# Attention's long step: attention-value products ahead of the mask products, bits compared in two halves, the second weight operation between them

## The chip, the cores and the metric

The kernel runs on one core of a Trainium2 chip. The metric is the device time of one execution in microseconds; the time before is the median of three runs. Engines are named as in the profile: PE is TensorE (PEld its weight loads), DVE is VectorE, ACT is ScalarE, POOL is GpSimd, SP is SyncE, which issues most of the transfers. The core has its own PSUM of eight banks, into which only TensorE's products go.

## What is computed

Attention over 2 x 8 heads, 768 positions and 64 numbers per head, in which a query sees a key only if both fall into the same bucket; the bucket is the set of signs of six projections. Two feed-forward blocks follow (squared ReLU, then SiLU), each with 512 inputs and 2048 hidden units.

```python
q_bits = (np.einsum('bhsd,dk->bhsk', q, proj) > 0).astype(np.int64)
k_bits = (np.einsum('bhsd,dk->bhsk', k, proj) > 0).astype(np.int64)
...
mask = q_bucket[:, :, :, None] == k_bucket[:, :, None, :]
scores = scale * np.matmul(q, k.transpose(0, 1, 3, 2))
scores = np.where(mask, scores, -1000000000.0)
...
return np.matmul(attn, v).astype(np.float32)
...
h = np.maximum(x @ w_in, 0.0)
return (h * h @ w_out).astype(np.float32)
...
g = h * (1.0 / (1.0 + np.exp(-h)))
return (g @ w_out).astype(np.float32)
```

## The kernel before

**The stages.** Attention comes first, then the two feed-forward blocks, whose order is set by a planner (`Plan`, `moe`) that the change does not touch. Attention is written out by hand: `manual_schedule` keeps every engine's instructions in the order in which the loop over `d` (L890) issues them. Each engine works its own list in order and waits at an instruction whose inputs aren't there.

**Units of work.** Heads are taken in pairs `p` (8 of them), a pair has four units `u` (head and half of the queries), a unit three groups of 128 queries `j`. A step `d` works on several stages at once. In the order of the loop:

- `row_max` (L683, VectorE) reads the scores that the step before produced, and `row_live` (L687, L688) prepares the scale and bias of the exponential.
- `t_lo` (L722, VectorE) and `t_hi` (L716, ScalarE) split a transposed tile of probabilities into a high and a low part. `transp` (L711, TensorE) makes the transposed tiles, two per step, three transposes each.
- `mid` holds VectorE's operations on the first block's weights, which arrive as 64-bit words: `w_exp` (L641) cuts the exponent to size, `w_sign` (L645) puts the sign in, `w_low` (L649) the low word. Before `w_exp`, `w_abs` runs on ScalarE (L633) and `w_limit` on GpSimd (L637).
- `score_exp` (L696, ScalarE) reads the scores out of PSUM and frees their buffer.
- `av` (L735, L736, TensorE) multiplies the values with the split probabilities, twice per step, two products each, for tiles that were transposed four tiles earlier. At a unit's end ScalarE copies the result out (L741).
- `score_mm` (L678, TensorE) computes the next scores in four products, two of which take the bits of the mask as further rows of queries and keys.

**The long steps.** `extra` adds work to eight of the steps. In steps 5, 17, 29, 41, 53, 65 and 77 `bits_mm` (L521) makes the six projections of the next pair's queries and keys, twelve products of 48 rows (six for each half `z` of the positions), into a tile `bs`. `bits_cmp` (L526, VectorE) compares them with zero and writes the bits `bt`. In steps 17 to 77, and alone in step 92, `rb_mm` (L758) transposes the reciprocals of an earlier pair's sums, and `x_norm` (L767, VectorE) multiplies the attention's output with them. The tiles `s`, `bs` and `rb` share two PSUM buffers (`ps_s`): the bit products wait until the exponential has read the one, the reciprocal transposes until it has read the other, and in steps 17 to 77 the step's own score products take the buffer of `bs` once the comparison has read it.

**Behind the comparison.** `place_bits` (L602) has SyncE copy the twelve bit rows to the operands `qq` and `kk` of the pair's first head right in the long step. The scores that need them are those of two steps later. GpSimd issues the loads of the pair after that (`load_hi`, L484 and L485); the second takes the place of the data that the bit products read.

**In a long step before the change** the loop issues all products of `extra` ahead of `av`, the comparison behind them, and the normalisation behind `av`; all weight operations of `mid` stand at the step's start. `mid` has three of them in step 17 (exponent, sign, low word), two in steps 29, 53 and 77 (exponent, sign), one in steps 41 and 65 (low word), none in steps 5 and 92.

Of the kernel before, what the change touches and what calls it, by code (L numbers as in the profile page):

```python
# [17 lines left out]
ALU = mybir.AluOpType  # L18
# [8 lines left out]
QW = 384  # L27
# [406 lines left out]
def lsh_attention_moe_moe(ctx, tc, kd, qk, v, pc, wi1, wo1, wi2, wo2, out):  # L434
    nc = tc.nc
# [31 lines left out]
    tm = [pcr[:, 2 * PW + 24 + 2 * i : 2 * PW + 26 + 2 * i] for i in range(3)]  # L467
# [46 lines left out]
    def bits_mm(p):  # L514
# [6 lines left out]
                mm(s[0:48, z, 0:QW], w, x[:, z * QW : (z + 1) * QW], start=j == 0, stop=j == 5)  # L521
        return s

    def bits_cmp(s, p):
        bt = pair[p]["bt"] = a1.tile([128, S], F32R, tag="bt", name=f"bt{p}")
        nc.vector.tensor_scalar(  # L526
            out=bt[0:48].rearrange("p (a b) -> p a b", a=2),
            in0=s[0:48, :, 0:QW],
            scalar1=tm[0][0:48, 0:1],
            scalar2=tm[0][0:48, 1:2],  # L530
            op0=ALU.is_gt,
            op1=ALU.mult,
        )


    first = {}
# [134 lines left out]
    def score_mm(u, j):  # L671
        p, h, z = u // 4, (u // 2) % 2, u % 2
        t = pair[p]
        s = ps_s.tile([128, 2, 512], F32, tag="s", name=f"s{u}_{j}")
        c0 = z * QW + j * 128
        for ab, kk in ((0, 128), (1, 64 + NBR)):
            for n in range(2):
                mm(s[:, n, 0:QW], t["qq"][h][0:kk, ab, c0 : c0 + 128], t["kk"][h][0:kk, ab, n * QW : (n + 1) * QW], start=ab == 0, stop=ab == 1)  # L678
        return s

    def row_max(u, j, s):
        m = mt[:, (u * 3 + j) % 4]
        nc.vector.tensor_reduce(out=m[:, 0:1], in_=s[:, :, 0:QW], op=ALU.max, axis=AX.XY, negate=True)  # L683
        return m

    def row_live(m):
        nc.vector.tensor_scalar(out=m[:, 1:2], in0=m[:, 0:1], scalar1=LIM, scalar2=1.0, op0=ALU.is_lt, op1=ALU.mult)  # L687
        nc.vector.tensor_scalar(out=m[:, 2:3], in0=m[:, 0:1], scalar1=LIM, scalar2=m[:, 0:1], op0=ALU.is_lt, op1=ALU.mult)  # L688

    def score_exp(u, j, s, m):  # L690
        p = u // 4
        if u % 4 == 0 and j == 0:
            sums[p] = a2.tile([128, 12], F32, tag="sums", name=f"sums{p}")
        e = P[u, j] = ac.tile([128, S], F32, tag="P", bufs=6, name=f"P{u}_{j}")
        c = (u % 4) * 3 + j
        nc.scalar.activation(  # L696
            out=e.rearrange("p (a b) -> p a b", a=2),
            in_=s[:, :, 0:QW],
            func=AF.Exp,
            scale=m[:, 1:2],  # L700
            bias=m[:, 2:3],
            accum_out=sums[p][:, c : c + 1],
        )
# [3 lines left out]
    def transp(g):  # L707
        u, kt = divmod(g, KT)
        t = ps_t.tile([128, 512], F32, tag="t", name=f"t{g}")
        for j in range(3):  # L710
            nc.tensor.transpose(t[:, j * 128 : (j + 1) * 128], P[u, j][:, kt * 128 : (kt + 1) * 128], ident)  # L711
        PT[g] = (t,)

    def t_hi(g):
        th = a1.tile([128, QW], F32R, tag="th", bufs=6, name=f"th{g}")
        nc.scalar.copy(out=th, in_=PT[g][0][:, 0:QW])  # L716
        PT[g] += (th,)

    def t_lo(g):
        t, th = PT[g]  # L720
        tl = a1.tile([128, QW], F32R, tag="tl", bufs=6, name=f"tl{g}")
        nc.vector.tensor_tensor(out=tl, in0=t[:, 0:QW], in1=th.bitcast(F32), op=ALU.subtract)  # L722
        PT[g] = th, tl
# [3 lines left out]
    def av(g):  # L727
        u, kt = divmod(g, KT)
        p, h, z = u // 4, (u // 2) % 2, u % 2
        if kt == 0:  # L730
            otile[u] = ps_o.tile([128, 512], F32, tag="o", name=f"o{u}")
        o = otile[u]
        vv = pair[p]["vv"][:, h * KT + kt].rearrange("p a d -> p (a d)")
        th, tl = PT.pop(g)
        mm(o[:, 0:QW], vv, th, start=kt == 0, stop=False)  # L735
        mm(o[:, 0:QW], vv, tl, start=False, stop=kt == KT - 1)  # L736
        if kt == KT - 1:
            if p not in xs:
                xs[p] = [a1.tile([128, S], F32, tag=n, bufs=b, name=f"{n}{p}") for n, b in (("ta", 2), ("tb", 1))]
            ob = a2.tile([128, QW], F32, tag="ob", name=f"ob{u}")  # L740
            nc.scalar.copy(out=ob, in_=o[:, 0:QW])  # L741
            for i in range(2):
                nc.sync.dma_start(out=xs[p][i][64 * h : 64 * h + 64, z * QW : (z + 1) * QW], in_=ob[64 * i : 64 * i + 64])
# [44 lines left out]
    extra = defaultdict(list)  # L788
    mid = defaultdict(list)
# [48 lines left out]
    with tc.manual_schedule():  # L838
# [12 lines left out]
        def warm_up(n):  # L851
            for _ in range(n):
                mm(warm, zb[:, 0:128], zb[:, 0:512], start=True, stop=True)
# [36 lines left out]
        for d in range(-5, G // 2 + 3):  # L890
            ready, new = new, None
            g = 2 * d
            if ready:
                m = row_max(*ready)
            if 0 <= g - 1 < G:
                t_lo(g - 1)
            if ready:
                row_live(m)
            for fn, a in mid.pop(d, []):
                fn(a)  # L900
            if 0 <= g < G:
                transp(g)
                t_hi(g)
                t_lo(g)
                transp(g + 1)
                t_hi(g + 1)
            more = extra.pop(d, [])
            if ready and more:
                score_exp(*ready, m)
            held = [(dve, pe(p), p) for pe, dve, p in more]  # L910
            for dve, t, p in held[:1]:
                dve(t, p)
            for n in (g - V_LAG, g + 1 - V_LAG):
                if 0 <= n < G:
                    av(n)
            for dve, t, p in held[1:]:
                dve(t, p)
            if ready and not more:
                score_exp(*ready, m)
            u, j = divmod(d + 5, 3)  # L920
            if u < NU:
                new = u, j, score_mm(u, j)
            if d < -1:
                warm_up(2)
            for fn, a in todo.pop(d, []):
                fn(*a)
# [3 lines left out]
        p = NPAIR - 1  # L930
        for z in range(2):
            t = ps_t.tile([128, 512], F32, tag="t", name=f"rb{p}_{z}")
# [13 lines left out]
        t = dict(x0=x0, ys=ys, xa=xa, wp=wp, raw=raw, wt=wt, src=((wi1, wo1), (wi2, wo2)), out=out)  # L946
# [51 lines left out]
```

## Time and profile before

| | |
|---|---|
| Median of three runs | 764.95 us (762.88 to 766.0) |
| Profiled execution | 764.35 us, its span 762.6 us |
| Busy: PE, PEld, DVE, ACT, POOL | 742.7, 627.7, 598.5, 456.8, 406.2 us |
| Chain that ended last, by engine | PE 74%, DVE 17%, DMA 3%, ACT 2%, issue 2% |
| Granted TensorE clock, mean | 0.998 |

The span goes from the first to the last instruction. A busy time adds up an engine's instructions, whose ends overlap the starts of the next; two numbers of a timeline row are the start and the duration, so the distance to the next start is what an instruction costs in a full queue. The bracket at a row's end tells how long the engine had been idle and what released it. Attention ends at about 255 us of the span.

### The profile page before, as it was taken

The page shows a single profiled execution, that of the slowest core. Times are in us where ns is not written, and L with a number is a line of the kernel's source. Part 1 is how long each engine was busy: PE and PEld are TensorE (multiplying, and loading weights), DVE is VectorE, ACT ScalarE, POOL GpSimd, SP SyncE. Part 2 cuts the span into 40 slices and gives each one's busy share as a digit, 9 for nine tenths or more (in the row PEclk, how much of TensorE's full clock was granted, in tenths as well). Part 3 has the DMA queues.
Part 4 walks back from the last instruction along what each step waited for, and adds up shares of the span by engine and source line. Part 5 has one row for each costly group of instructions (what it writes and reads, how often), then busy time and mean ns, then how long its engine had stood idle before and what let it go on. Part 6 is the DMA issues. An engine that isn't in the chain of part 4 may idle for free.

```text
span 762.6 us, 10898 instructions
## 1 busy us (share of the span) xinstructions
PE 742.7 (97%) x3748; PEld 627.7 (82%) x3748; DVE 598.5 (78%) x1064; ACT 456.8 (60%) x856; POOL 406.2 (53%) x295
## 2 busy tenths in 40 slices
PE   7989999999999989999999999999999999999998
PEld 3688988989988878888888888888788888888887
DVE  4989999999999899658748966899975875685542
ACT  4777978888979766367268239446634625623520
POOL 3454464863754674753564662867567256455200
PEclk9999999999999999999999999999999999999999
DMA  5496976876851402221221211102222031121012
GB/s 150 127 230 162 218 186 162 212 201 154 217 124 36 168 28 83 83 83 56 83 79 60 83 58 50 61 28 80 88 83 83 25 113 32 53 93 45 1 69 97
DMA packets 29398, 77.09 MB, mean 101 GB/s; under 512 B 4432, under 2 KB 8912, under 8 KB 29344
## 3 DMA queue, kind: packets, MB, share of 16 engines
q1 hardware_dynamic: 25152, 64.99, 29.2%
q0 software_dynamic: 4032, 11.01, 6.2%
q8 instruction: 30, 0.49, 0.3%
q10 hardware_dynamic: 160, 0.39, 0.2%
q14 instruction: 24, 0.20, 0.1%
HBM read 52.15 MB, written 3.15 MB: 73 GB/s over the span
## 4 chain that ended last, share of the span: by engine, by line
PE 74%; DVE 17%; DMA 3%; ACT 2%; issue 2%; POOL 1%; SPq 1%; DVEq 0%; ACTq 0%
PE bank L336 32%; PE bank L255 16%; PE bank L226 9%; PE s L678 5%; DVE mt L683 4%; PE t L711 4%; DVE tl L722 3%; PE o L735 2%; PE o L736 2%; DVE ys L149 2%; PE bs L521 2%; ACT P L696 1%; DVE xb L155 1%; DVE ts L260 1%; DMA ta<-ob 1%
## 5 line engine op out<-in xcount | busy, mean ns | idle before, releaser
L170 POOL TENSOR_SCALAR wt<-wt 128x512 f32<-128x512 f32 x56 | 117.1, 2100 | 45.2 <-ACT wt L168 45.2
L155 POOL TENSOR_TENSOR wp<-wt,wp 128x512 fp32r<-128x512 f32 x56 | 76.6, 1379 | 96.1 <-ACT wp L153 96.1
L255 PE MATMUL bank<-xb,wp 128*128 128x512 f32 x480 | 111.3, 390 | 2.4 <-DVE ts L260 1.6
L696 ACT ACTIVATE P<-s,mt 128x768 f32<-128x768 f32 x96 | 95.6, 996 | 23.6 <-DVE mt L688 20.9
L255 PEld LDWEIGHTS bank<-xb,wp 128*128 128x128 f32 x480 | 89.7, 188 | 22.6 <-issue 1.5
L722 DVE TENSOR_TENSOR tl<-t,th 128x384 fp32r<-128x384 f32 x192 | 104.7, 547 | 1.8 <-ACT th L716 1.6
L683 DVE TENSOR_REDUCE mt<-s 128x1 f32<-128x768 f32 x96 | 91.3, 951 | 8.7 <-PE s L678 8.3
L153 ACT CAST wp<-wt 128x512 fp32r<-128x512 f32 x56 | 34.6, 620 | 105.7 <-DVE wt L173 64.4
L716 ACT CAST th<-t 128x384 fp32r<-128x384 f32 x192 | 82.2, 483 | 22.4 <-PE t L711 22.3
L678 PE MATMUL s<-kk,qq 76*128 76x384 f32 (+1 forms) x384 | 85.2, 341 | 6.1 <-DMA kk<-bt 2.1
L711 PE MATMUL t<-ident,P 128*128 128x128 f32 x576 | 81.7, 274 | 2.0 <-DVE tl L722 1.9
L260 DVE TENSOR_TENSOR ts<-bank,ts 128x512 f32<-128x512 f32 x80 | 54.5, 690 | 36.8 <-PE bank L255 34.2
L226 PE MATMUL bank<-x0h,wp 128*128 128x512 f32 x256 | 80.2, 389 | 0.0
L678 PEld LDWEIGHTS s<-kk,qq 76*128 76x128 f32 (+1 forms) x384 | 67.6, 188 | 10.2 <-issue 5.4
L711 PEld LDWEIGHTS t<-ident,P 128*128 128x128 f32 x576 | 67.6, 140 | 10.1 <-DVE tl L722 4.3
L735 PE MATMUL o<-th,vv 128*128 128x384 f32 x192 | 72.4, 377 | 0.1
L736 PE MATMUL o<-tl,vv 128*128 128x384 f32 x192 | 64.6, 337 | 0.0
L240 ACT ACTIVATE ts<-bank 128x512 f32<-128x512 f32 x48 | 28.6, 595 | 52.1 <-PE bank L226 26.6
L226 PEld LDWEIGHTS bank<-x0h,wp 128*128 128x128 f32 x256 | 48.1, 188 | 10.0
L155 DVE TENSOR_TENSOR gql<-ts,gqh 128x512 fp32r<-128x512 f32 x64 | 46.2, 733 | 12.7 <-ACT gqh L153 12.4
L172 DVE SCALAR_TENSOR_TENSOR wt<-raw,wt 128x512 uint32<-128x512 uint32 x58 | 51.5, 890 | 0.6
L168 ACT ACTIVATE wt<-raw 128x512 f32<-128x512 f32 x58 | 38.7, 669 | 20.6 <-POOL wp L155 11.0
(153 smaller groups left out, 1707.1 us busy)
## 6 DMA issues: line engine op xcount, KB each, us to landing
raw<-in_dram SPq DMA_DIRECT2D x64, 512.0 KB
qq<-hq SPq DMA_DIRECT2D x28, 192.0 KB
kk<-in_dram POOLq DMA_DIRECT2D x14, 384.0 KB, 5.0
vr<-in_dram SPq DMA_DIRECT2D x8, 384.0 KB
ta<-ob SPq DMA_DIRECT2D x32, 96.0 KB
tb<-ob SPq DMA_DIRECT2D x32, 96.0 KB
out_dram<-ts SPq DMA_DIRECT2D x11, 256.0 KB
rq<-in_dram SPq DMA_DIRECT2D x7, 384.0 KB
```

The lines of the kernel that those rows point to most:

```text
L155: add(("DVE", "POOL")[pool], l, lambda: eng.tensor_tensor(out=lo(), in0=src(), in1=hi().bitcast(F32), op=ALU.subtract), (*rk, *hk), lk)
L170: add("DVE" if fast else "POOL", 0.5 if fast else 2.4, lambda: eng.tensor_scalar(out=wtt, in0=wtt, scalar1=W_LO, scalar2=W_HI, op0=ALU.max ...
L226: mm(bank[b], w[:, x, op, sl], t["x0"][y][:, kt], start=kt == 0 and j == 0, stop=kt == 3 and j == 2)
L255: mm(bank[b], w[:, p, op, k * 128 : k * 128 + 128], x[:, q, xop, k], start=first and k == 0 and j == 0, stop=k == 1 and j == 2, skip_group ...
L336: mm(bank[b][:, 0:wd], x, y, start=i == 0 and n == 0, stop=i == FB - 1 and n == 2)
L678: mm(s[:, n, 0:QW], t["qq"][h][0:kk, ab, c0 : c0 + 128], t["kk"][h][0:kk, ab, n * QW : (n + 1) * QW], start=ab == 0, stop=ab == 1)
L683: nc.vector.tensor_reduce(out=m[:, 0:1], in_=s[:, :, 0:QW], op=ALU.max, axis=AX.XY, negate=True)
L696: nc.scalar.activation(out=e.rearrange("p (a b) -> p a b", a=2), in_=s[:, :, 0:QW], func=AF.Exp, scale=m[:, 1:2], bias=m[:, 2:3], accum_ou ...
L711: nc.tensor.transpose(t[:, j * 128 : (j + 1) * 128], P[u, j][:, kt * 128 : (kt + 1) * 128], ident)
L716: nc.scalar.copy(out=th, in_=PT[g][0][:, 0:QW])
L722: nc.vector.tensor_tensor(out=tl, in0=t[:, 0:QW], in1=th.bitcast(F32), op=ALU.subtract)
L735: mm(o[:, 0:QW], vv, th, start=kt == 0, stop=False)
```

## The change

`av` comes ahead of the products of `extra`, so that in a long step the order on TensorE is transposes, attention-value products, bit products, reciprocal transposes, scores. Both kinds of `extra` work are now issued as products first and VectorE work behind them. The comparison becomes two instructions of 384 columns, one per half of the positions. In a long step the weight operations of `mid` from the second on are kept back in a list `between` and issued after the first half.

```diff
+    between = []
+
     def bits_cmp(s, p):
         bt = pair[p]["bt"] = a1.tile([128, S], F32R, tag="bt", name=f"bt{p}")
-        nc.vector.tensor_scalar(
-            out=bt[0:48].rearrange("p (a b) -> p a b", a=2),
-            in0=s[0:48, :, 0:QW],
-            scalar1=tm[0][0:48, 0:1],
-            scalar2=tm[0][0:48, 1:2],
-            op0=ALU.is_gt,
-            op1=ALU.mult,
-        )
+        for z in range(2):
+            nc.vector.tensor_scalar(
+                out=bt[0:48, z * QW : (z + 1) * QW],
+                in0=s[0:48, z, 0:QW],
+                scalar1=tm[0][0:48, 0:1],
+                scalar2=tm[0][0:48, 1:2],
+                op0=ALU.is_gt,
+                op1=ALU.mult,
+            )
+            while between:
+                fn, a = between.pop(0)
+                fn(a)
...
             if ready:
                 row_live(m)
-            for fn, a in mid.pop(d, []):
-                fn(a)
+            more = extra.pop(d, [])
+            for i, (fn, a) in enumerate(mid.pop(d, [])):
+                if more and i:
+                    between.append((fn, a))
+                else:
+                    fn(a)
             if 0 <= g < G:
                 transp(g)
                 t_hi(g)
                 t_lo(g)
                 transp(g + 1)
                 t_hi(g + 1)
-            more = extra.pop(d, [])
             if ready and more:
                 score_exp(*ready, m)
-            held = [(dve, pe(p), p) for pe, dve, p in more]
-            for dve, t, p in held[:1]:
-                dve(t, p)
             for n in (g - V_LAG, g + 1 - V_LAG):
                 if 0 <= n < G:
                     av(n)
-            for dve, t, p in held[1:]:
+            for dve, t, p in [(dve, pe(p), p) for pe, dve, p in more]:
                 dve(t, p)
```

The lists below name the lines of the kernel that they belong to; behind the comparison the changed kernel's lines are six further down. The bracket says for which engine's or queue's results an instruction waits at its start.

TensorE in step 17, before, from the last transpose to the score products (`o` is the attention-value product, `rb` the reciprocals; seven rows of the bit products are left out):

```order
L711 MATMUL t_894<-ident,P_2_761 128x128
L521 MATMUL bs_902<-hq_489,pjh 48x384 [waits DMASW3_49,Activation_49]
L521 MATMUL bs_902<-hq_489,pjl 48x384
L521 MATMUL bs_902<-lp_601,pjh 48x384
...
L521 MATMUL bs_902<-hk_490,pjl 48x384
L521 MATMUL bs_902<-lp_601,pjh 48x384
L758 MATMUL rb_915<-ident,rw_809 128x128 [waits PE_49,Activation_49,Pool_49]
L735 MATMUL o_924<-th_820,vv_485 128x384
L736 MATMUL o_924<-tl_822,vv_485 128x384
L678 MATMUL s_1_930<-kk_1_561,qq_1_560 128x384 [waits DVE_49]
```

The same place after the change:

```order
L717 MATMUL t_893<-ident,P_2_762 128x128
L741 MATMUL o_901<-th_821,vv_486 128x384 [waits Activation_49]
L742 MATMUL o_901<-tl_823,vv_486 128x384
L521 MATMUL bs_906<-hq_490,pjh 48x384 [waits DMASW3_49,Activation_49]
L521 MATMUL bs_906<-hq_490,pjl 48x384
...
L521 MATMUL bs_906<-hk_491,pjl 48x384
L521 MATMUL bs_906<-lp_602,pjh 48x384
L764 MATMUL rb_919<-ident,rw_810 128x128 [waits PE_49,Activation_49,Pool_49]
L684 MATMUL s_1_932<-kk_1_562,qq_1_561 128x384 [waits DVE_49]
```

The attention-value products moved from between the reciprocals and the scores to directly behind the transposes; the scores, which wait for VectorE, now stand directly behind the reciprocals.

VectorE in step 17, before, from the first weight operation (`wi`) to the normalisation (`ta` from `rb`):

```order
L641 TENSOR_SCALAR wi_304<-wi_304 128x512 [waits Pool_49]
L645 SCALAR_TENSOR_TENSOR wi_304<-raw_67,wi_304 128x512 [waits DMAHW5_49,DVE_49]
L649 SCALAR_TENSOR_TENSOR wi_304<-raw_67,wi_304 128x512 [waits DVE_49]
L722 TENSOR_TENSOR tl_892<-t_886,th_890 128x384 [waits Activation_49]
L526 TENSOR_SCALAR bt_922<-bs_902,pcr 48x768 [waits DMAHW6_49,DMAHW5_49,DMAHW7_49,DMAHW4_49,PE_49]
L767 TENSOR_TENSOR ta_424<-rb_915,ta_424 128x768 [waits DMAHW2_49,DMAHW0_49,DMAHW3_49,PE_49,Pool_49]
```

The same place after the change:

```order
L647 TENSOR_SCALAR wi_304<-wi_304 128x512 [waits Pool_49]
L728 TENSOR_TENSOR tl_891<-t_885,th_889 128x384 [waits Activation_49]
L529 TENSOR_SCALAR bt_926<-bs_906,pcr 48x384 [waits DMAHW6_49,DMAHW5_49,DMAHW7_49,DMAHW4_49,PE_49]
L651 SCALAR_TENSOR_TENSOR wi_304<-raw_67,wi_304 128x512 [waits DVE_49]
L655 SCALAR_TENSOR_TENSOR wi_304<-raw_67,wi_304 128x512 [waits DVE_49]
L529 TENSOR_SCALAR bt_926<-bs_906,pcr 48x384
L773 TENSOR_TENSOR ta_424<-rb_919,ta_424 128x768 [waits DMAHW2_49,DMAHW0_49,DMAHW3_49,PE_49,Pool_49]
```

The sign and low-word operations moved from ahead of the split `tl` to between the two halves of the comparison; only the first half has a wait for TensorE.

## Rows read from the trace of the kernel before

**Rows 1.** Busy time by stretch: stretch, its length, PE, PEld, DVE, ACT, POOL, clock, DMA share, GB/s

```profile
71.00:95.00 24.00, 23.73 (x160) 22.48 (x159) 23.08 (x58) 21.29 (x48) 13.22 (x13) 1.00 1.02 223
250.00:762.60 512.60, 507.10 (x2255) 419.29 (x2254) 372.52 (x530) 257.91 (x427) 272.17 (x164) 1.00 0.20 68
```

**Rows 2.** Waits from 30 to 260 us: us in total, times, longest

```profile
PE bs L521 <- ACT P L696: 2.6, 7, 0.6
PE s L678 <- issue: 1.5, 3, 0.8
```

**Rows 3.** Timeline of step 41: start, us, engine, line, operation; PE, then DVE

```profile
124.18 0.82 PE L711 MATMUL t<-ident,P 128*128 128x128 f32 x6
125.19 0.38 PE L521 MATMUL bs<-hq,pjh 128*48 128x384 f32 x1 [0.19 <-ACT P L696]
...
127.13 0.34 PE L521 MATMUL bs<-lp,pjh 128*48 128x384 f32 x1
...
127.88 0.42 PE L735 MATMUL o<-th,vv 128*128 128x384 f32 x1
...
128.66 0.94 PE L678 MATMUL s<-kk,qq 128*128 128x384 f32 x4
129.44 0.82 PE L711 MATMUL t<-ident,P 128*128 128x128 f32 x6
130.02 0.42 PE L735 MATMUL o<-th,vv 128*128 128x384 f32 x1
...
127.51 1.07 DVE L526 TENSOR_SCALAR bt<-bs,pcr 48x768 fp32r<-48x768 f32 x1 [0.47 <-PE bs L521]
```

**Rows 4.** Timeline of step 53: PE, then DVE

```profile
153.29 0.93 PE L711 MATMUL t<-ident,P 128*128 128x128 f32 x6
154.82 0.38 PE L521 MATMUL bs<-hq,pjh 128*48 128x384 f32 x1 [0.60 <-ACT P L696]
...
158.29 0.95 PE L678 MATMUL s<-kk,qq 128*128 128x384 f32 x4
...
155.50 0.69 DVE L645 SCALAR_TENSOR_TENSOR wi<-raw,wi 128x512 uint32<-128x512 uint32 x1
...
157.14 1.07 DVE L526 TENSOR_SCALAR bt<-bs,pcr 48x768 fp32r<-48x768 f32 x1 [0.48 <-PE bs L521]
```

**Rows 5.** Timeline near the start: the first pair's comparison, two halves in a row

```profile
20.81 1.27 DVE L596 TENSOR_SCALAR qq<-bf,pcr 12x384 fp32r<-12x384 f32 x2
```

**Rows 6.** Timeline of step 17: PE, then DVE

```profile
66.07 0.38 PE L521 MATMUL bs<-hq,pjh 128*48 128x384 f32 x1 [0.19 <-ACT P L696]
...
70.15 0.97 PE L678 MATMUL s<-kk,qq 128*128 128x384 f32 x4 [0.44 <-DVE bt L526]
...
67.23 0.69 DVE L645 SCALAR_TENSOR_TENSOR wi<-raw,wi 128x512 uint32<-128x512 uint32 x1
67.96 0.69 DVE L649 SCALAR_TENSOR_TENSOR wi<-raw,wi 128x512 uint32<-128x512 uint32 x1
68.57 0.55 DVE L722 TENSOR_TENSOR tl<-t,th 128x384 fp32r<-128x384 f32 x1
69.03 1.06 DVE L526 TENSOR_SCALAR bt<-bs,pcr 48x768 fp32r<-48x768 f32 x1
```

**Rows 7.** Timeline of step 29, DVE: the exponent operation

```profile
97.91 0.43 DVE L641 TENSOR_SCALAR wi<-wi 128x512 uint32<-128x512 uint32 x1 [1.67 <-POOL wi L637]
```

**Rows 8.** Bits on their way: chain that ended last (step 5), then timelines (steps 41 to 43, step 19)

```profile
40.73 5.06 DMA kk<-bt
...
128.87 0.55 POOL L485 DMA_DIRECT2D hk<-in_dram  x1
134.14 0.59 PE L678 MATMUL s<-kk,qq 76*128 76x384 f32 x2 [0.78 <-issue]
...
74.37 1.12 PE L678 MATMUL s<-kk,qq 128*128 128x384 f32 x4
```

**Rows 9.** Timeline of step 92, DVE: the last normalisation in the loop

```profile
248.37 0.95 DVE L767 TENSOR_TENSOR ys<-rb,ta 128x768 f32<-128x768 f32 x1
```

## The prediction, made before the changed kernel ran

> **What bounds the kernel now.** I read three views. The stretches come first: between long steps TensorE is busy 23.73 of 24.00 us and VectorE 23.08, and after the attention stage TensorE is busy 507.10 of 512.60 us [rows 1]. So inside attention two engines are full at once, and a delay at the end of attention has almost no idle time behind it in which to vanish: I carry it to the end one to one. The list of waits comes second: TensorE sat idle 2.6 us in all before the bit products, seven times, for the exponential that frees their PSUM buffer, and 1.5 us in three waits that the trace ascribes to "issue" [rows 2]. The timelines of the long steps come third; the reader should follow one of them.
>
> Take d = 41 [rows 3]. Six transposes, a wait of 0.19, twelve bit products (1.94 us from the first start to the last), six transposes of the reciprocals, four attention-value products (0.78), the score product, then the next step's transposes. The comparison starts 0.38 us after the last bit product and takes 1.07. The score product needs the comparison's end, since it writes the buffer that the comparison reads. It began at 128.66, and the comparison ended at 127.51 + 1.07 = 128.58. So before the change, the four attention-value products hide the comparison.
>
> **Part 1, the attention-value products go ahead.** They start behind the transposes: 124.18 + 0.58 (transposes to attention-value, from 129.44 to 130.02) = 124.76, and end 0.78 later, at 125.54. The bit products began at 125.19, so they start 0.35 later [rows 3]. The wait for the exponential disappears, but the cover over the comparison does too. Steps 5, 17 and 65 have the same wait of 0.19 or 0.20. In steps 53 and 77 that wait was 0.60: 153.29 + 0.58 + 0.78 = 154.65 lies before 154.82, and the bit products do not move [rows 4]. The reciprocal transposes move with the bit products and end before the score is released, so they cost nothing; their cover is the comparison's new wait.
>
> **Part 2, the comparison in halves.** Two back-to-back instructions of 384 columns took 1.27 us in this trace (12 partitions instead of 48) [rows 5]; one of 768 takes 1.07 [rows 3]: 0.20 more. I take 0.20. By the Trainium skill ("Perfetto Trace Analysis", section "Optimizing Scalar/DVE Operations") the overhead of an instruction that reads PSUM is about 0.125 us; by that figure my sum would be some 0.4 us lower. The split would earn something if the first half started after the sixth bit product. The list of the changed program says otherwise: the first half waits for TensorE, the second for nothing. As the second needs the twelfth product, the wait of the first must already cover it. So I let neither half start earlier than the whole did.
>
> **Part 3, weight operations between the halves.** Before, the sign operation ran ahead of the comparison, in time in which VectorE waited for the bit products anyway. The comparison at 157.14 had 0.48 of such waiting left [rows 4]. Now it stands behind that wait, ahead of the second half, and the score needs that half. One such operation is 0.61 to the next instruction (67.96 to 68.57), and 0.73 when the next one reads its result (67.23 to 67.96) [rows 6]. The freed VectorE time is in front of the first half, where nothing can use it.
>
> **End of the comparison, step by step.**
> - Steps 5, 41, 65 (nothing between): 0.35 + 0.20 = 0.55 later. The score of step 41 starts 0.06 behind it (as 69.03 + 1.06 = 70.09 to 70.15 in [rows 6]): 129.19, 0.53 later. In step 5 the score takes the other buffer and comes 0.35 earlier, but the copies of the bits go out later.
> - Steps 53, 77 (sign between): 157.14 + 1.27 + 0.61 = 159.02 against 158.21, 0.81 later; score at 159.08 against 158.29, 0.79 later.
> - Step 17 (sign and low word between): the first half at 66.07 + 0.35 + 1.94 + 0.38 = 68.74, the end at 68.74 + 1.27 + 0.73 + 0.61 = 71.35 against 70.09: 1.26 later, the score too.
> - Step 29: the exponent operation waited 1.67 for GpSimd [rows 7], so all VectorE work comes late and in line with it, in either order: only the 0.20.
>
> **What of it lasts.** Behind the comparison, SyncE copies the bits to both operands, and the score two steps later waits for the copies. In step 5 that copy takes 5.06 us to land and lies on the chain that ended last; in step 43 TensorE waits 0.78 for it, in steps 55 and 67 0.35 each (the rest of the 1.5 in [rows 2]), in step 19 the score is 0.18 longer than in step 41 (1.12 against 0.94) [rows 3, 8]. Such a wait absorbs part of the delay, unless the copies land later by as much. Landing is the unknown: 5.06 from one issue in step 5, while in step 43 it falls 5.27 us behind GpSimd's load of the next pair (128.87 to 134.14) [rows 8], which goes out when TensorE's bit products are over. If that load sets the landing, it moves by 0 to 0.35; if the copies' own issue does, by the comparison's delay. My terms, with both ends:
> - step 5: 0 to 0.55, taken 0.28, halfway, as no row decides
> - step 17: 1.26 less 0.18 = 1.08 to 1.26, taken 1.10
> - step 29: 0.20
> - step 41: 0 to 0.55, taken 0.45, between 0.35 and 0.55
> - step 53: 0.79 less 0.35 = 0.44 to 0.81, taken 0.50
> - step 65: 0.53 less 0.35 = 0.18 to 0.55, taken 0.45
> - step 77: no wait two steps later, 0.79
> - step 92, reciprocal transposes alone, 0.78 later: the normalisation at 248.37 stood directly behind another VectorE instruction, not behind TensorE [rows 9], so 0 to 0.78, taken 0.25
>
> The sum is 4.0 us, with ends at 2.7 and 5.5. The profiled execution took 764.35, so 768.35 by its own time; the median of the runs is 0.60 higher, and my forecast of **769.0 us** (0.5% slower) stands on the median, 764.95. A measurement of this kernel can tell about 0.5% (3.8 us) from no change, and the forecast lies on that bound.
>
> **Rivals.**
> - *The load sets the landing* (not slower by the bound). GpSimd's load of the next pair occupies the DMA engines, and the small copies land when it is through, whenever they were issued. Steps 5, 41 and 65 then lose 0 to 0.2 and the waits absorb the rest: +2.7, 767.6. It decides wherever the copies' own delay is under what the load still needs. For it: the landings of [rows 8] are long for twelve rows of 768 four-byte numbers. Against it: in steps 17, 53 and 77 the score is late by more than any wait there. By the Trainium skill ("DMA: Bandwidth & Descriptors", section "Anatomy of one DMA") a transfer costs about 2.0 us plus its bytes at 436 GB/s, an estimated 2.1 us here; the trace disagrees with 5.06 [rows 8], which speaks for other traffic.
> - *The copies move with the comparison.* All upper ends: +5.5, 770.4.
> - *The halves are released apart.* The first half starts after the sixth product, 6 x 1.94 / 11 = 1.06 us earlier, and only the second half (half of 1.27, 0.64) follows the last. In step 41 the comparison then ends at 127.13 + 0.35 + 0.38 + 0.64 = 128.50, 0.1 earlier than before; in step 53 the chain from the first half at 157.14 - 1.06 ends at 156.08 + 0.64 + 0.61 + 0.64 = 157.97, 0.2 earlier. Three steps gain 0.1, two gain 0.2, steps 17 and 29 still lose 0.20 each and step 92 0.25: 0.65 less 0.7, no change, 764.9. It decides by one thing, whether the first wait names the sixth or the twelfth product; the missing wait of the second half speaks against it. The same page section of the Trainium skill says that, where VectorE isn't saturated but causes bubbles elsewhere, breaking up instructions may let work finish sooner; [rows 1] show it nearly saturated, and the rule needs this earlier release.
> - *Faster beyond the bound* would need 3.8 us, more than all the 2.6 us of idle time that the move can remove [rows 2].
>
> **How the numbers follow.** The forecast's case 0.52, the load 0.24, the copies 0.16, the halves apart 0.06, faster 0.02. The forecast's own range of 3.3 to 4.8 us straddles the bound: a little over half of it is slower, with the copies' case and a tenth of the load's 0.49; same 0.49; faster 0.02. The range goes from 765.8 (2.7 on the median, less 1.8 for the scatter of the runs, which reached 2.1 below their median) to 771.5 (5.5, and 1.05 for the highest run).
>
> **What would show it.** Right: the bit products no longer wait for the exponential in steps 5, 17, 41, 65; the first half starts about 0.38 behind the twelfth product; the scores of six steps wait for the comparison, some 1.0 us in 41 and 65, 1.6 in 53 and 77, 2.3 in 17; step 17 is the longest. Wrong: a first half that starts while bit products still run, or scores of steps 53 and 77 no later than now. The waits two steps on tell the landing: if they shrink, the load sets it; if they keep their size, the copies do.

## The result and the profile after

| | before | after |
|---|---|---|
| Median of six runs each, alternating on one chip | 765.22 us (761.21 to 766.63) | 768.45 us (767.53 to 770.12) |
| Ratio, with its 95% interval | | 1.0059 [1.0038, 1.008] |
| Profiled execution, its span | 764.35, 762.6 us | 770.12, 768.3 us |
| Granted TensorE clock of that execution | 0.998 | 0.991 |

The change makes the kernel slower by 0.59%: 768.45 us measured, 769.0 forecast. (The ratio is an estimate over all twelve runs; the quotient of the two medians is 1.0042.) That the sum came out does not show that its terms did. The rest of this text takes them one by one, and a good part of the loss turns out to have a cause that the forecast did not have.

First the page of the kernel after: busy time, and the chain that ended last by engine.

```profile
PE 746.1 (97%) x3748; PEld 631.2 (82%) x3748; DVE 599.3 (78%) x1071; ACT 457.0 (59%) x856; POOL 406.3 (53%) x295
...
PE 85%; DVE 10%; DMA 2%; issue 1%; POOL 1%; ACT 0%; SPq 0%; DVEq 0%; ACTq 0%
```

TensorE's busy time grew from 742.7 to 746.1 us with the same products. The same work that takes longer means a slower clock; we come back to it. In the waits from 30 to 265 us the trade of the change can be read in a few lines. First the kernel before (TensorE, then VectorE):

```profile
PE s L678 <- DMA kk<-bt: 2.1, 1, 2.1
...
PE s L678 <- DVE bt L526: 1.4, 2, 1.0
...
DVE bt L526 <- PE bs L521: 3.0, 5, 1.1
```

Then the kernel after:

```profile
PE s L684 <- DVE bt L529: 7.3, 6, 2.0
PE s L684 <- DMA kk<-bt: 2.5, 1, 2.5
...
DVE bt L529 <- PE bs L521: 7.3, 7, 1.4
```

The 2.6 us in which the bit products waited for the exponential [rows 2] are gone from TensorE's list, as is the 1.5 us put down to "issue". In their place the scores wait 7.3 us in six steps for the second half of the comparison, where they waited 1.4 us in two steps (17 and 29) before. And VectorE waits 7.3 us ahead of the first half, where it waited 3.0 ahead of the whole comparison: most of the difference is time that the weight operations used to fill (without the third part it is 4.4).

The timeline of the kernel after, step 17 (TensorE, VectorE) and then step 41, answers to [rows 6] and [rows 3]:

```profile
71.39 0.34 PE L521 MATMUL bs<-lp,pjh 128*48 128x384 f32 x1
71.56 0.82 PE L764 MATMUL rb<-ident,rw 128*128 128x128 f32 x6
74.40 0.97 PE L684 MATMUL s<-kk,qq 128*128 128x384 f32 x4 [2.02 <-DVE bt L529]
...
77.31 1.48 PE L684 MATMUL s<-kk,qq 128*128 128x384 f32 x4
...
71.77 0.67 DVE L529 TENSOR_SCALAR bt<-bs,pcr 48x384 fp32r<-48x384 f32 x1 [1.02 <-PE bs L521]
72.36 0.67 DVE L651 SCALAR_TENSOR_TENSOR wi<-raw,wi 128x512 uint32<-128x512 uint32 x1
73.07 0.69 DVE L655 SCALAR_TENSOR_TENSOR wi<-raw,wi 128x512 uint32<-128x512 uint32 x1
73.68 0.66 DVE L529 TENSOR_SCALAR bt<-bs,pcr 48x384 fp32r<-48x384 f32 x1
...
132.21 0.34 PE L521 MATMUL bs<-lp,pjh 128*48 128x384 f32 x1
132.38 0.82 PE L764 MATMUL rb<-ident,rw 128*128 128x128 f32 x6
133.89 0.98 PE L684 MATMUL s<-kk,qq 128*128 128x384 f32 x4 [0.69 <-DVE bt L529]
...
132.58 1.25 DVE L529 TENSOR_SCALAR bt<-bs,pcr 48x384 fp32r<-48x384 f32 x2 [0.76 <-PE bs L521]
```

In step 17 the first half starts at 71.77, 0.38 behind the start of the twelfth bit product; the second ends at 74.34 with both weight operations in between, and the score follows 0.06 later. In step 41 the two halves take 1.25 us, 0.18 more than the whole comparison before (1.07). All of that is as forecast. Not forecast: the score of the next step, 77.31, takes 1.48 us instead of the 0.86 of an undisturbed one. The stretches of the kernel after say why (length, PE, PEld, DVE, ACT, POOL, granted clock, DMA share, GB/s):

```profile
47.00:48.00 1.00, 0.56 (x4) 0.55 (x5) 0.00 (x0) 0.00 (x0) 0.00 (x0) 1.00 1.28 230
48.00:49.00 1.00, 1.00 (x9) 1.00 (x7) 0.93 (x2) 0.51 (x2) 0.00 (x0) 0.68 1.12 218
49.00:50.00 1.00, 1.00 (x5) 1.00 (x5) 1.00 (x5) 0.74 (x2) 0.00 (x0) 0.50 1.09 267
50.00:51.00 1.00, 1.00 (x5) 1.00 (x4) 0.14 (x1) 0.80 (x2) 0.76 (x1) 0.50 1.08 211
...
75.00:76.00 1.00, 1.00 (x10) 0.97 (x8) 0.80 (x2) 0.21 (x1) 0.64 (x2) 0.84 0.86 280
76.00:77.00 1.00, 1.00 (x6) 1.00 (x5) 1.00 (x5) 0.75 (x2) 1.00 (x1) 0.50 0.47 129
77.00:78.00 1.00, 1.00 (x5) 1.00 (x5) 0.47 (x2) 0.95 (x2) 1.00 (x3) 0.50 0.68 129
78.00:79.00 1.00, 1.00 (x5) 0.90 (x4) 0.17 (x1) 0.13 (x2) 0.92 (x2) 0.50 1.00 369
```

Behind the 2.53 us in which TensorE waited for the copies in step 7, and behind the 2.02 us of step 17, the granted clock is 0.50 (the 1.2 GHz level) for some 3 us each, and each microsecond holds five or six matmul records instead of nine or ten.

In this execution the first feed-forward product starts 5.75 us later than before. Start-up is 1.02 us longer in it and is left out; the table shows where the other 4.73 us arise, from `row_max`'s start in one step to a later step, after less before:

| between steps | shift, us | forecast's term |
|---|---|---|
| 5 and 8 (copies of step 5) | +0.50 | 0.28 |
| 8 and 10 (half clock) | +1.56 | none |
| 17 and 18 (score of step 17) | +1.17 | 1.10 |
| 18 and 21 (half clock) | +1.29 | none |
| 28 and 30 | -0.76 | 0.20 |
| 41 and 44 | +0.49, then -0.97 | 0.45 |
| 53 and 56 | +0.79, then -0.54 | 0.50 |
| 65 and 68 | +0.47, then -0.52 | 0.45 |
| 77 and 78 | +0.81 | 0.79 |
| 91 and the first feed-forward product | +0.44 | 0.25 |

The table is one execution, and the slowest of the six, with the lowest granted clock (0.991; the others 0.993 to 0.995). The row of steps 5 and 8 is no fixed cost: in a second profile of the same kernel, in the section on the clock, that shift is -0.57 instead of +0.50.

So two theories went into the experiments. **Cover**: the scores come late because the comparison has lost its cover, and the copies of the bits with it. **Clock**: the two long idles bring the clock down, and that is much of the loss.

### The profile page after: what moved, and what is told of

The parts are those of the page before. It is cut to its first block, busy times and chain, and to the rows that moved or that the text cites. A ratio compares the mean times of both kernels' runs of the same rounds, so it can differ in the third digit from the quotient of the medians.

```text
span 768.3 us, 10904 instructions
## 1 busy us (share of the span) xinstructions
PE 746.1 (97%) x3748; PEld 631.2 (82%) x3748; DVE 599.3 (78%) x1071; ACT 457.0 (59%) x856; POOL 406.3 (53%) x295
## 4 chain that ended last, share of the span: by engine, by line
PE 85%; DVE 10%; DMA 2%; issue 1%; POOL 1%; ACT 0%; SPq 0%; DVEq 0%; ACTq 0%
PE bank L336 32%; PE bank L255 16%; PE bank L226 8%; PE s L684 8%; PE t L717 8%; PE o L741 4%; PE o L742 4%; DVE ys L149 2%; PE bs L521 2%; DVE xb L155 1%; DVE ts L260 1%; DVE bt L529 1%; PE warm L859 1%; DMA kk<-bt 1%; DVE wt L172 1%
```

## The parts alone

The runs below came in three sets, each beside the kernel before on one chip; its medians were 764.06, 764.41 and 764.20 us.

**Attention-value products first, nothing else.** In the loop of the kernel before:

```
-            held = [(dve, pe(p), p) for pe, dve, p in more]
-            for dve, t, p in held[:1]:
-                dve(t, p)
             for n in (g - V_LAG, g + 1 - V_LAG):
...
-            for dve, t, p in held[1:]:
+            for dve, t, p in [(dve, pe(p), p) for pe, dve, p in more]:
```

> Alone from the change: the attention-value products ahead of the bit products. The comparison stays whole, all weight operations stay at the step's start. Theory 'cover' (the time comes from scores that start later because the comparison ends later): the comparison ends 0.35 us later in steps 5, 41 and 65, not later in 17, 29, 53 and 77, so scores of 41 and 65 start 0.35 later and the wait two steps later takes that back; step 92 costs about 0.4 as in the changed kernel. In all 0.4 to 1.0 us over the kernel before, ratio about 1.001. Theory 'clock' (most of the change's time comes from two stretches at half clock, in steps 7 to 9 and 17 to 19, that follow long idle stretches of TensorE): the idle ahead of step 7's masked score grows from 2.1 to about 2.4 us; if that suffices, the granted clock is 0.5 in steps 8 and 9 and the time is 1.6 us more, 2 to 2.6 us in all; step 17 keeps its clock.

Measured: 764.71 us, ratio 1.0019 [1.0002, 1.0036]. That is about what *cover* expected. The idle ahead of step 7's masked score did not grow to 2.4 us as expected, it was 1.49, so this run says nothing on *clock*.

**The split, nothing else.** The loop `for z in range(2)` of the change in `bits_cmp`, without the weight operations in it.

> Alone from the change: the comparison in two halves, back to back; order of the products and of the weight operations as before. Theory 'cover': the comparison ends 0.2 us later in each of seven steps, the scores of six start 0.1 to 0.2 later, the waits two steps on take back three of these: 0.4 to 1.0 us over the kernel before. Theory 'clock': the idle stretch ahead of step 7's masked score is 2.1 to 2.3 us, with none at half clock behind it: the same 0.4 to 1.0, clock as in the kernel before.

Measured: 764.65 us, ratio 1.0006 [0.9987, 1.0025]. Both theories expected this time, and it can't be told from no change.

**The split with the weight operations in it, old order of the products.** The change without its last two hunks on `held`.

> The comparison in halves with the weight operations between them, but the products in the old order (attention-value products behind the reciprocals). Theory 'cover': the comparison ends 0.9 us later in step 17, 0.8 in 53 and 77, 0.2 in the others: 1.5 to 2.5 us over the kernel before, less what waits take back. Theory 'clock': as TensorE has 0.78 us of attention-value products left while it would wait, its idle in step 17 is about 1.3 us instead of 2.0, no half clock follows there, and the time is 0.5 to 1.5 us over the kernel before.

Measured: 766.19 us, ratio 1.0026 [1.001, 1.0041], some 2 us, as *cover* expected (1.5 to 2.5); *clock* had 0.5 to 1.5.

**The first two parts together, without the third:**

```
-                if more and i:
+                if False:
                     between.append((fn, a))
```

> The kernel after without its third part: attention-value products ahead of the bit products and the comparison in two halves, but the weight operations ahead of the comparison as in the kernel before. If the parts add, its ratio is that of the two parts alone, 1.0019 and 1.0006, so 1.0025 (766.3), and the third part is worth the rest, 0.0030; in its profile the scores of steps 41 and 65 come 0.5 us late, those of 53 and 77 0.2 us, that of step 17 0.2 to 0.4 us, and step 7 is as in the kernel after. If the third part matters only by the long idle of step 17 and the clock behind it, the ratio is nearer 1.0045.

Measured: 764.80 us, ratio 1.0013 [0.999, 1.0035]. TensorE's waits there:

```profile
PE s L684 <- DVE bt L529: 4.5, 6, 1.0
PE s L684 <- DMA kk<-bt: 1.6, 1, 1.6
```

What follows: scores that wait 4.5 us for the comparison cost at most 0.35% in the run without the third part, and its centre is at 0.13%. The delays of the single scores agree with the forecast in these profiles (step 41: 0.30 with the first part alone, 0.19 with the split; step 53: 0.80 with split and weight operation, none of it from the first part), but the waits two steps on take much of it back: from step 41 to 44 this run first loses 0.48 and then wins 0.97. Of the expectation's two values, 1.0025 (the parts add) lies inside the interval and 1.0045 (the third part matters only by the clock) outside. The split with the third part has an interval clear of zero, 0.1 to 0.4%. The whole change has 0.0053 to 0.0059, so the third part is worth 0.0040 to 0.0046 on top of the first two, and 0.0020 in the old order (1.0026 less 1.0006). From the intervals of the runs, each of these differences is known to some 0.003 only, so it is likely but not shown that the third part costs more where it meets the first. The profiles show what would do it: with the first part the score of step 17 waits 2.02 us, against 1.31 in the run with the old order, whose clock stayed at 1.00.

## The clock

**The long idles filled.** The kernel after with matmuls that nothing reads in the two idles: seven repeated pairs of the first score products in step 7, and the reciprocals' transposes of step 17 four times.

```
+        for n in [0, 1] * (7 if (u, j) == (4, 0) else 0):
+            mm(s[:, n, 0:QW], t["qq"][h][:, 0, c0 : c0 + 128], t["kk"][h][:, 0, n * QW : (n + 1) * QW], start=True, stop=True)
...
+        for _ in range(4 if p == 0 else 1):
```

> The changed kernel, with TensorE kept at work in its two longest idle stretches by repeated products that change no result: in step 7 the first pair of score products 7 times more (about 2.4 us), in step 17 the reciprocal transposes 3 times more (about 1.7 us). Theory 'clock': no stretch at half clock in steps 8, 9, 18 and 19, 2.5 to 3 us under the changed kernel, so 765.5 to 766, ratio to the kernel before 1.001 to 1.002. Theory 'cover': scores and copies come as in the changed kernel, so its time, 768 to 769, ratio 1.005, within 0.5 us.

Measured: 767.46 us, ratio 1.0039 [1.0024, 1.0055]. The clock no longer fell in either place:

```profile
40.00:52.00 12.00, 11.94 (x77) 11.28 (x76) 9.51 (x24) 8.67 (x20) 7.96 (x7) 1.00 1.03 233
64.00:80.00 16.00, 15.95 (x112) 14.85 (x111) 14.76 (x35) 11.14 (x26) 8.72 (x12) 1.00 0.59 158
```

The time fits neither expectation: some 1 us came back, where *clock* expected 2.5 to 3 and *cover* at most 0.5. The 2.5 to 3 went by the first profile, which had both falls; the second profile of that kernel, below, has one.

**A long idle in the old order.** The kernel before with pair 1's first copies behind the load of the values in SyncE's queue:

```
-        at(d0 + 5, place_bits, p, 0)
+        at(d0 + (6 if p == 1 else 5), place_bits, p, 0)
```

> The kernel before with one thing moved: the two copies of pair 1's bits that are issued in step 5 stand behind the load of the values in SyncE's queue instead of ahead of it. Nothing in the comparison, the weight operations or the order of the products changes. In the kernel before, the masked score product of step 7 waited 2.09 us for these copies and the granted clock stayed at 1.00 behind it. Both theories expect this wait to grow, to 3 to 4.5 us. The clock theory (a long idle of TensorE brings the granted clock to one half for some 3 us) expects 0.50 in the microseconds behind it, with score products of 1.48 us instead of 0.86, and a loss of 1.5 us beside the longer wait: 766.5 to 768. The cover theory (the half clock belongs to something in the changed order) expects 1.00 throughout and the longer wait alone: 765.3 to 766.5.

Measured: 766.66 us, ratio 1.0025 [1.0005, 1.0044]. The wait grew to 3.51 us, and the clock fell while it lasted and stayed low behind it. First the timeline of this run, then its stretches:

```profile
47.35 0.98 PE L678 MATMUL s<-kk,qq 76*128 76x384 f32 x2 [3.51 <-DMA kk<-bt]
...
50.68 1.48 PE L678 MATMUL s<-kk,qq 128*128 128x384 f32 x4
```

```profile
46.00:48.00 2.00, 0.65 (x2) 0.69 (x3) 0.00 (x0) 0.00 (x0) 1.92 (x3) 0.50 1.30 198
48.00:50.00 2.00, 2.00 (x10) 1.90 (x9) 1.64 (x5) 0.78 (x2) 2.00 (x2) 0.50 1.17 206
50.00:52.00 2.00, 2.00 (x8) 1.90 (x8) 0.43 (x1) 1.16 (x3) 1.21 (x1) 0.50 1.05 246
```

The time is just inside what *clock* expected (766.5 to 768). Four of the six runs have a mean clock of 0.993 and 766.4 to 767.1 us, the other two have 0.998 and 764.08 and 765.05, so the clock hardly fell in these. The copies themselves went out at the same times as in the kernel before (39.8 and 40.7 us). Only the load of the values, 384 KB, now goes ahead of them, and they landed 1.4 us later: with the issue unchanged, it is the other traffic that sets the landing here.

**The kernel after once more,** unchanged:

> The kernel after, unchanged, beside the others on one chip, so that these can be set against it. Expected: 1.004 to 1.007 of the kernel before; a wait of about 2.5 us in step 7 and 2.0 us in step 17, and if the clock theory is right granted clocks of 0.50 behind both again; 1.00 there if the two half-clock stretches of the first profile were chance.

Measured: 768.30 us, ratio 1.0053 [1.0036, 1.007]. This time step 7 waited 1.48 us and kept its clock; step 17 waited 2.01 us and lost it:

```profile
70.79 1.54 PE L684 MATMUL s<-kk,qq 128*128 128x384 f32 x4 [2.01 <-DVE bt L529]
```

```profile
72.00:74.00 2.00, 2.00 (x10) 1.90 (x9) 1.63 (x5) 0.78 (x2) 1.92 (x4) 0.50 0.72 168
```

What follows: the half clock belongs to the idle and not to the changed order, since the old order shows it too once its idle is 3.51 us, and the changed order no longer shows it once its idles are filled. How much of the loss is it? Every run lists its mean granted clock, so runs with the same value can be set against each other. At 0.993 the kernel before has a median of 766.1 us (11 runs) and the kernel after 768.7 (8 runs, both sets): 2.6 more. At 0.995 it is 764.6 (8 runs) and 767.3 (3 runs): 2.7 more. Between the medians of all these runs, 764.21 us (85 runs of the kernel before, those beside the experiments) and 768.45 us (12), lie 4.2 us. I read the 2.6 as what the later work costs at equal clock, and the remaining 1.6 as the lower clock (an estimate): its mean over the runs is 0.9933 after and 0.9963 before. The filled version fits: its mean is 0.9967, that of the kernel before, and it still loses 0.39%, some 3 us. How the 1.6 divides between the steps and the start-up, whose clock also varies from run to run, is open.

## The cover

**The halves truly apart.** The kernel after, with the bit products in two tiles of the transpositions' ring, one for each half, and the second low part of the step ahead of the comparison:

```
-        s = ps_s.tile([128, 2, 512], F32, tag="s", name=f"bs{p}")
+        s = [ps_t.tile([128, 512], F32, tag="t", name=f"bs{p}_{z}") for z in range(2)]
...
             if ready and more:
                 score_exp(*ready, m)
+                t_lo(g + 1)
+                lo_done = True
```

> The kernel after, with the bit products of the two halves in two tiles of the transpositions' ring instead of one tile of the scores' ring; the second low part of the step is computed ahead of the comparison, so that the next step's transpositions find their tile free. Each half of the comparison then waits for its own six products, and no score takes a tile that the comparison has to free. The theory of the late comparison (the first half waits for all twelve products, and the scores wait for the second half) expects the first half 0.9 to 1.0 us earlier, against the last bit product, than in the kernel after; the six waits of the scores for the comparison (7.3 us) gone; and, since a part of what is won is given back where copies land and in the waits two steps on, 762 to 765.5 in all, at least 3 us below the kernel after. The rival (the loss of the kernel after comes from copies that land late and from the clock alone, and the scores' waits are absorbed) expects the waits gone and the time within 1 us of the kernel after: 767 to 769.

Measured: 764.00 us, ratio 0.9987 [0.9974, 1.0]; 4.3 us below the kernel after on the same chip. The timeline of this run's step 17:

```profile
69.30 0.34 PE L521 MATMUL bs<-lp,pjh 128*48 128x384 f32 x1
...
70.52 0.82 PE L764 MATMUL rb<-ident,rw 128*128 128x128 f32 x6
71.09 0.94 PE L684 MATMUL s<-kk,qq 128*128 128x384 f32 x4
...
69.68 0.66 DVE L529 TENSOR_SCALAR bt<-bs,pcr 48x384 fp32r<-48x384 f32 x1
70.27 0.67 DVE L651 SCALAR_TENSOR_TENSOR wi<-raw,wi 128x512 uint32<-128x512 uint32 x1
70.98 0.69 DVE L655 SCALAR_TENSOR_TENSOR wi<-raw,wi 128x512 uint32<-128x512 uint32 x1
71.59 0.66 DVE L529 TENSOR_SCALAR bt<-bs,pcr 48x384 fp32r<-48x384 f32 x1
```

The first half now starts 0.38 behind the sixth product (69.30 to 69.68) while the other six still run, and the score at 71.09 starts behind the transposes of the reciprocals without waiting, ahead of the second half's end. No score waits for the same weight operations between the same two halves here. What made them dear is thus what the kernel after shares: both halves and the score depended on all of one tile. This run changes three things at once, the own tile of each half, with it the tile that the score takes, and the earlier low part; which of them gives more was not separated. Its granted clock is 0.9963 in the mean, against 0.9937 in the six runs of the kernel after beside it, so a part of the 4.3 us is clock.

**One step earlier as well,** first with the weight operations of steps 17, 29 and the like held back to the next comparison, behind what reads them (the first block's weights are then other numbers, the work the same), then with these in place:

```
-        extra[d0 + 5].append((bits_mm, bits_cmp, p))
+        extra[d0 + 4].append((bits_mm, bits_cmp, p))
...
-        at(d0 + 5, place_bits, p, 0)
+        at(d0 + 4, place_bits, p, 0)
```

> As the run with the halves apart, and the bit products, the comparison and the first head's copies of every pair one step earlier (steps 4, 16, 28 and so on instead of 5, 17, 29); the products that spread the row sums stay where they are, and the weight operations too. If the landing of the copies is what holds step 7 and its like (2.5 us in step 7 of the kernel after, and smaller waits in the others), those waits fall to 0 to 0.5 us, since each copy is issued about 2.7 us earlier: 2 to 3 us below the run with the halves apart, 759.5 to 763. If landing depends on the other transfers and not on the time of issue, the waits stay and it comes out within 1 us of the run with the halves apart. Both expect the granted clock at 1.00 in these steps where no idle is over 2 us.

> The halves apart and one step earlier, with the weight operations held back only in steps that have a comparison; in e7_apart_step_earlier those of steps 17, 29 and the like were held back to the next comparison, too late for what reads them. The same work otherwise, so both theories expect the time of that run, 761 to 763, the attention part some 5.5 us shorter than in the kernel before and no idle over 1 us in it; if the late weight operations were what made that run quicker, 763 to 765.

Measured: 761.77 us, ratio 0.9965 [0.9951, 0.9978], and with the weight operations in place 762.34 us, ratio 0.9979 [0.9963, 0.9996]. In the second run the wait for the copies is down to 0.2 us:

```profile
PE s L684 <- ACT P L702: 2.8, 6, 0.5
...
PE s L684 <- DMA kk<-bt: 0.2, 1, 0.2
```

The second of these beats the kernel before by 0.21%, and is some 6 us below the kernel after. The earlier step and the own tiles apart, its loop and its amount of work are those of the change. Its time is as expected, its attention is not: the first feed-forward product comes 1.6 us earlier than in the kernel before, where I had expected an attention some 5.5 us shorter.

**One step earlier without the own tiles,** in the order of the change and in that of the kernel before:

> The kernel after with bit products, comparison and first copies of each pair one step earlier, in the scores' ring as before, the products that spread the row sums left where they are. The bit products and those products then stand in different steps, so a score takes the tile of the score before it and waits for that one's exponential, which is issued early, not for the comparison. If the order of the change (attention-value products first, halves, weight operations) costs time only because the score stands behind the comparison and the copies land late, its loss goes: 761 to 764, no wait of a score for the comparison, and within 1.5 us of the run with the halves apart one step earlier. If the order itself costs, 765 to 767.

> The kernel before with the same move by one step: bit products, one comparison, first copies. Beside e11_after_step_earlier it tells what the change is worth where no score waits for the comparison. If the change costs by the late scores alone, the two agree within 1 us, 761 to 764 both. If the bit products at the front of the step, ahead of the attention-value products, wait for the exponential there (0.2 to 0.6 us in each of seven steps), this one is 1 to 3 us slower than e11_after_step_earlier.

Measured: 768.22 us, ratio 1.0044 [1.0025, 1.0062], and 766.34 us, ratio 1.0024 [1.0005, 1.0042]. Both expectations failed. No score waits for the comparison, yet in both runs six scores have another wait, of 1.25 us each in the first and 0.79 in the second. Here is step 41 of the first:

```profile
128.15 0.82 PE L764 MATMUL rb<-ident,rw 128*128 128x128 f32 x6
...
130.22 0.97 PE L684 MATMUL s<-kk,qq 128*128 128x384 f32 x4 [1.25 <-ACT P L702]
...
128.97 0.67 DVE L655 SCALAR_TENSOR_TENSOR wi<-raw,wi 128x512 uint32<-128x512 uint32 x1
129.08 0.99 ACT L702 ACTIVATE P<-s,mt 128x768 f32<-128x768 f32 x1 [0.85 <-DVE mt L694]
```

A ring of two that takes one extra tile in a step gives the step's score the tile of the score just before it, and the exponential that frees that tile has only begun at 129.08. With two extra tiles in one step, as in both kernels of the study, the score takes the bits' tile. I had counted the wait that goes and not asked which tile comes next.

That is not all of their loss. From `row_max`'s first start to the first feed-forward product, the profile of the first run is 1.1 us longer than that of the kernel before, and that of the second 0.4 us *shorter*. Behind attention the first then loses 1.8 us more and the second 1.5: VectorE waits for the last output of attention, and TensorE for VectorE. The kernel before, then two rows of the first run:

```profile
259.78 1.02 DVE L936 TENSOR_TENSOR ys<-rb,ta 128x384 f32<-128x384 f32 x2 [1.74 <-POOL ta L763]
```

```profile
264.57 1.02 DVE L942 TENSOR_TENSOR ys<-rb,ta 128x384 f32<-128x384 f32 x2 [3.54 <-POOL ta L769]
...
277.29 1.88 PE L255 MATMUL bank<-xb,wp 128*128 128x512 f32 x7 [2.59 <-DVE xb L155]
```

The second run has 3.10 and 2.12 us at these two places; in every other profile the first is 1.73 to 1.75 us, and the second 0.75 to 0.80. Why the last output comes later in these two is open, so they do not tell what the change is worth without the wait for the comparison.

## Why the prediction was right, and where it was not

- **Right: the order of events.** Neither half starts before the twelfth product; in steps 5, 17, 41 and 65 the bit products no longer wait; six scores wait for the comparison, and the wait of step 17 is the longest of them. The run with the halves apart is the counter-test: with a tile each, the first half starts behind the sixth product.
- **Right: the delays of the scores.** Forecast 1.26, 0.53, 0.79, 0.53 and 0.79 in steps 17, 41, 53, 65 and 77, measured 1.17, 0.49, 0.79, 0.47 and 0.81. The waits I had named for them (1.0, 1.6, 2.3) were each 0.3 too long (0.69, 1.30, 2.02): I had let them begin 0.58 behind the start of the reciprocals' transposes, and the trace lets these run for 0.82.
- **Wrong: "What of it lasts".** The terms of steps 29, 41, 53 and 65, 1.60 in sum, measured -0.76, -0.48, +0.25 and -0.05. The waits two steps on (0.78, 0.35, 0.35 of the 1.5 in [rows 2]) did not shrink, they vanished, and in step 29 VectorE's wait for GpSimd [rows 7] went from 1.67 to 0.14 us: everything came later, and GpSimd's result was there.
- **Which landing.** By the prediction's own test the vanished waits speak for the rival *the load sets the landing*, which I had given 0.24. The profiles say the same: where a score of steps 43, 55 or 67 had to wait, in the kernel before and in five of the runs, it started 4.8 to 5.3 us behind GpSimd's load, but anything from 3.8 to 4.7 behind the issue of the copy to `kk`. The rival's +2.7 is close to the 2.6 that the kernel after loses at equal clock, but not term by term: it had +0.20 for step 29 and nothing below zero for step 41. The table of shifts without its two half-clock rows gives 1.88, for one execution. For the landing itself, the prediction takes an estimate of 2.1 us from the Trainium skill ("DMA: Bandwidth & Descriptors", section "Anatomy of one DMA"). That section is about transfers that GpSimd issues, and SyncE issues these copies; no term of the sum rests on it.
- **Missing: the clock.** No term and no rival spoke of it, though the prediction itself named idles of over 2 us (2.3 in step 17) on an engine whose granted clock the page lists. 2.85 us of that execution's 4.73 are this. Between the medians it is less: about 1.6 of the 4.2 by the comparison at equal clock, and some 1 us came back when the two idles were filled.
- So the forecast of 4.0 met a loss of about 4 (4.5 by the ratio, 4.2 between the medians of all runs) by luck, through two errors that cancel: some 1.4 too much for the lasting delays, and nothing for the clock.
- *The halves are released apart* was a rival with 0.06 at 764.9, no change. The kernel that has that release measured 764.0 beside 764.41. That is near the price, but the run also has the score's other tile, so it does not test the terms; and the change did not contain this release.

## What to carry to other kernels

Splitting an instruction let its consumer start sooner here only where each half had its own producer to wait for. Two halves of one tile that a single wait guards were one instruction with 0.18 us more to pay, and anything put between them delayed whoever waited for the tile. Before moving cover away from a dependency, look up which buffer the next product takes and what frees it, for this step and for the one after. And on TensorE an idle of the length of these (2 us and more) may cost again behind its end: look at the granted clock of the stretches there before adding up waits alone.

## What the runs showed of the hardware

The granted clock fell to 0.50 (the 1.2 GHz level) with idles of TensorE of 2.01, 2.02, 2.53 and 3.51 us, for 3 to 7 us. It stayed at 1.00 behind an idle of 2.09 us in step 7 of the kernel before:

```profile
45.92 0.59 PE L678 MATMUL s<-kk,qq 76*128 76x384 f32 x2 [2.09 <-DMA kk<-bt]
```

```profile
40.00:52.00 12.00, 9.91 (x69) 9.45 (x67) 9.57 (x22) 8.54 (x19) 9.36 (x7) 1.00 1.16 275
```

And it stayed at 1.00 behind one of 2.53 us in step 7 of the run with the halves apart:

```profile
47.53 0.59 PE L684 MATMUL s<-kk,qq 76*128 76x384 f32 x2 [2.53 <-DMA kk<-bt]
```

```profile
49.00:51.00 2.00, 2.00 (x15) 1.97 (x14) 2.00 (x6) 1.61 (x5) 1.84 (x2) 1.00 1.40 184
```

Behind attention, the last two runs give one case each way: the idle of 2.12 us at 275 us brought the clock down (0.54 in the two microseconds behind it), that of 2.59 us at 277 us did not.

So the length of the idle alone does not decide. The Trainium skill ("TensorE: Matmul & The Clock Gate", Part 1) says that the monitor that sets the clock is free-running and does not reset when a kernel starts, and that the moment at which the clock rises varies by this from run to run. That it matters in the same way where an idle falls is my inference from it: the two outcomes at 2.53 us agree with that, and no run here shows it.
